# Windowed attention into a two-layer feed-forward block: V loaded and shifted by pairs, weights after it, y products 24 slots behind

## The chip, the cores and the metric

The kernel runs on one core of a Trainium2 chip. The metric is the device time in microseconds of one execution. TensorE (PE, with its weight loads on PEld), VectorE (DVE), ScalarE (ACT) and GpSimd (POOL) run their own instruction streams in order; SyncE (SP) and POOL issue the transfers here, each in its own queue order. SP's transfers form queue q1 of the profile, POOL's form queue q0, and both run on the core's 16 DMA engines.

## The reference

For 8 batches, 8 heads, 576 positions and a head size of 64 (inputs in float32):

```python
scores = scale * np.matmul(q, k.transpose(0, 1, 3, 2))
rel = pos[:, None] - pos[None, :]
mask = (rel >= 0) & (rel < window)          # window = 64
attn = softmax(np.where(mask, scores, -1e9))
attn_out = np.matmul(attn, v)
x = attn_out.transpose(0, 2, 1, 3).reshape(B * S, H * D)   # 4608 x 512
h = x @ w_in                                # 512 -> 2048
g = h - np.tanh(h)
y = g @ w_out                               # 2048 -> 512
```

## The kernel before

**Attention.** A pair g is two heads of one batch (heads pr and pr + 4 of batch b, g = 4b + pr), so there are 32 pairs. Every window of 64 queries sees its own 64 keys and the 64 before it, so 9 windows make a pair. For each pair SP loads q and k (`load_qk`, 288 KB each), an engine casts them to bf16 (`cast_qk`, on POOL but for pair 0), PE transposes them (`tr`, tiles `tp`), ACT and DVE copy the transposes out (`qt`, `kt`), PE makes the scores in three groups of three windows (`scores`, `sp`), ACT takes the exponential (`pt`), DVE multiplies by the mask, PE multiplies by V in three groups (`pv`, tile `ov`), and DVE normalises into `xs` (`rc`, then two multiplications for each group). After every second pair PE transposes two pairs' `xs` (`x_tr`, tile `tpx`, first windows 0 to 3, then 4 to 8) and DVE copies them into `xT`, the input of the first layer. `tp` and `tpx` share a pool of two PSUM buffers.

**V.** A tile `vw` for one batch (two such tiles, batches take turns) holds on partitions 64 to 127 the V rows of a window and on partitions 0 to 63 those of the window before. `load_v` fills the upper half from DRAM with a cast to bf16, in two transfers on POOL's queue, in pieces of 64 elements (128 B); `shift_v` copies the upper half to the lower, one window further, on SP's queue. No `pv` group can finish before both.

**Feed-forward.** The 4608 tokens are 9 chunks of 512 and d_ff is 16 tiles of 128. For chunk c and tile m, `hp_mm` makes four matmuls (`hp`), ACT the tanh (`th`) and DVE the difference (`gT`). `yp_mm` makes four matmuls of the second layer (`yp`); four of these make 128 tokens of output, which ACT copies (`ysb`, `y_out`) and SP stores. `yp` has one PSUM buffer.

**Order.** Everything is written out by half-slots h; slot n is half-slots 2n and 2n + 1. An even half-slot holds one `hp_mm`, an odd one a `yp_mm`; the attention's pieces are put at half-slots by tables (`TIGHT` for batches 0 and 1, `WIDE` for the rest), counted from a start a that depends on the pair. Slots 0 to 143 hold the first layer's 9 x 16 `hp_mm`; the second layer runs 16 slots behind it (slots 16 to 159). All of batch 0's attention stands ahead of slot 0, batch 1's pairs start at half-slots 8, 12, 16 and 20 (its first `pv` in slot 7), and batch 2's pairs at half-slots 20, 28, and so on.

**Start.** POOL issues in this order: V of batch 0 (pair 0, then pairs 1 to 3 together), the four quarters of w_in among the casts of pairs 1 to 3, the four quarters of w_out, V of batch 1, V of batch 2, then the casts of the following pairs. SP issues q and k of pairs 0 to 3, the shift of batch 0 (pair 0, then the rest), q and k of later pairs, the shift of batch 1 in one transfer. A transfer waits on its queue until the transfer eight places ahead on that queue has landed, since eight semaphores take turns.

Of the kernel before, what the change touches and what calls it, by code (L numbers as in the profile page):

```python
# [15 lines left out]
def kernel(  # L16
# [9 lines left out]
    nc = tc.nc  # L26
    B, H, S, D = q.shape
    NP = H // 2
# [7 lines left out]
    NC = NT // TOK  # L36
    M = d_ff // 128
# [2 lines left out]
    ctx.enter_context(tc.manual_schedule())  # L40

    const = ctx.enter_context(tc.tile_pool(name="const", bufs=1))
    qk_pool = ctx.enter_context(tc.tile_pool(name="qk", bufs=5))
    row_pool = ctx.enter_context(tc.tile_pool(name="row", bufs=3))
    sm_pool = ctx.enter_context(tc.tile_pool(name="sm", bufs=3))
    xt_pool = ctx.enter_context(tc.tile_pool(name="xt", bufs=3))
    g_pool = ctx.enter_context(tc.tile_pool(name="g", bufs=2))
    ps_hp = ctx.enter_context(tc.tile_pool(name="ps_hp", bufs=2, space=PSUM))
    ps_yp = ctx.enter_context(tc.tile_pool(name="ps_yp", bufs=1, space=PSUM))
    ps_tp = ctx.enter_context(tc.tile_pool(name="ps_tp", bufs=2, space=PSUM))  # L50
# [4 lines left out]
    mask = const.tile([128, 64], BF16, name="mask")  # L55
    w_in_sb = const.tile([128, 4, d_ff], BF16, name="w_in_sb")
    w_out_sb = const.tile([128, M, d_model], BF16, name="w_out_sb")
# [17 lines left out]
    def cast(eng, g, n):  # L75
        t = row_pool.tile([P, E, 2, D], BF16, tag=n + "b", name=n + "b")
        o = t.rearrange("p e h d -> p h e d")
        i = stage.pop((g, n)).rearrange("p h (e d) -> p h e d", d=D)
        if eng is nc.scalar:
            nc.scalar.activation(o, i, ACT.Copy)  # L80
        else:
            eng.tensor_copy(o, i)  # L82
        rows[g, n] = t

    def cast_qk(g):
        cast(nc.gpsimd, g, "q")
        cast(nc.gpsimd, g, "k")

    def load_v(b, p0=0, p1=NP):
        for i in range(2):  # L90
            nc.gpsimd.dma_start(  # L91
                out=vw[b % NV][64:128, p0:p1, :, 64 * i:64 * i + 64].rearrange("p r j d -> p (r j) d"),
                in_=v[b, NP * i + p0:NP * i + p1].rearrange("h (j p) d -> p (h j) d", p=64))

    def shift_v(b, p0=0, p1=NP):
        w = vw[b % NV].rearrange("p r j c -> p r (j c)")
        nc.sync.dma_start(out=w[0:64, p0:p1, 129:], in_=w[64:128, p0:p1, :(NJ - 1) * 129])


    for g in range(NP):  # L100
        load_qk(g)
# [7 lines left out]
    for i in range(NR):  # L109
        nc.vector.memset(qT[i], 0.0)  # L110
        nc.vector.memset(kT[i][:, 0:64], 0.0)
    nc.gpsimd.memset(mask, 1.0)

    nc.gpsimd.affine_select(mask, mask, compare_op=ALU.is_ge, fill=0.0,
                            base=-1, pattern=[[-1, 8], [-8, 8]], channel_multiplier=1)
    nc.gpsimd.affine_select(mask, mask, compare_op=ALU.is_ge, fill=0.0,
                            base=64, pattern=[[1, 8], [8, 8]], channel_multiplier=-1)
    w_in_r = moe_w_in.rearrange("(ko ki) f -> ki ko f", ki=128)
    w_out_r = moe_w_out.rearrange("(ko ki) f -> ki ko f", ki=128)

    def load_w_in(i):
        nc.gpsimd.dma_start(out=w_in_sb[:, :, 512 * i:512 * i + 512],
                            in_=w_in_r[:, :, 512 * i:512 * i + 512])

    def load_w_out(i):
        nc.gpsimd.dma_start(out=w_out_sb[:, 4 * i:4 * i + 4, :], in_=w_out_r[:, 4 * i:4 * i + 4, :])

    cast(nc.scalar, 0, "q")
    cast(nc.vector, 0, "k")
    load_v(0, 1, NP)  # L130
    load_w_in(0)
    cast_qk(1)
    load_w_in(1)
    cast_qk(2)
    load_w_in(2)
    load_w_in(3)
    cast_qk(3)
    for i in range(4):
        load_w_out(i)
    load_v(1)  # L140
    shift_v(0, 0, 1)
    shift_v(0, 1, NP)

    xT = {}

# [64 lines left out]
    def hp_mm(c, m):  # L210
        hp = ps_hp.tile([128, TOK], F32, tag="hp", name="hp")
        for ki in range(4):
            nc.tensor.matmul(hp, w_in_sb[:, ki, m * 128:(m + 1) * 128], chunk_tile(c)[:, ki, :],  # L213
                             start=(ki == 0), stop=(ki == 3))
        th = sm_pool.tile([128, TOK], F32, tag="th", name="th")
        nc.scalar.activation(th, hp, ACT.Tanh)  # L216
        return hp, th

    def g_sub(c, m, hp, th):
        if m == 0:  # L220
            gT[c] = g_pool.tile([128, M, TOK], BF16, tag="gT", name="gT")
        nc.vector.tensor_tensor(gT[c][:, m, :], hp, th, ALU.subtract)  # L222

    def yp_mm(c, st):
        s, part = divmod(st, 4)
        if part == 0:
            yps[c, s] = ps_yp.tile([128, d_model], F32, tag="yp", name="yp")
        for i in range(4):
            m = 4 * part + i
            nc.tensor.matmul(yps[c, s], gT[c][:, m, s * 128:(s + 1) * 128], w_out_sb[:, m, :],  # L230
                             start=(m == 0), stop=(m == M - 1))

    def y_out(c, s):
        ysb = sm_pool.tile([128, d_model], F32, tag="ysb", name="ysb")
        nc.scalar.activation(ysb, yps[c, s], ACT.Copy)  # L235
        for u in range(2):
            r0 = c * TOK + s * 128 + 64 * u
            nc.sync.dma_start(out=out[r0:r0 + 64, :].rearrange("(a e) d -> e a d", e=E),
                              in_=ysb[64 * u:64 * u + 64, :])
# [3 lines left out]
    items = {}  # L243

    def at(h, *fn):
        items.setdefault(h, []).append(fn)

    NG = B * NP
    WIDE = dict(q=0, k=1, s0=4, s1=4, s2=6, mask=8, v0=10, v1=13, v2=15, x0=17, x1=19)
    TIGHT = dict(q=0, k=1, s0=3, s1=3, s2=4, mask=5, v0=6, v1=7, v2=8, x0=10, x1=11)  # L250
    at_v2 = {}
    for g in range(NG):
        b, pr = divmod(g, NP)
        o = TIGHT if b < 2 else WIDE
        a = 3 * g - 21 if b == 0 else 4 * g - 8 if b == 1 else 8 * g - 44
        if b > 0:
            at(a - 24, load_qk, g)
            at(a - 8, cast_qk, g)
        at(a + o["q"], tr, g, "q")
        at(a + o["k"], tr, g, "k")  # L260
        for i in range(3):
            at(a + o[f"s{i}"], scores, g, i)
        at(a + o["mask"], masking, g)
        for i in range(3):
            at(a + o[f"v{i}"], pv, g, i)
        at_v2[g] = a + o["v2"]
        if pr % 2 == 1:
            at(a + o["x0"], x_tr, b, pr // 2, 0, 4)
            at(a + o["x1"], x_tr, b, pr // 2, 4, NJ)
    at(6, shift_v, 1)  # L270
    for b in range(2, B):
        a = at_v2[NP * (b - 1) - 1] + 1
        at(a, load_v, b)
        at(a + 22, shift_v, b)

    for h in range(min(items), 2 * 16 * (NC + 1) + 2):
        n = h // 2
        c, m = divmod(n, M)
        if h % 2 == 0:
            cy, sy = divmod(n - 17, M)  # L280
            if n >= 17 and sy % 4 == 3 and cy < NC:
                y_out(cy, sy // 4)
            if 0 <= c < NC:
                hidden = hp_mm(c, m)
        elif 1 <= c <= NC:
            yp_mm(c - 1, m)
        for fn in items.get(h, []):
            fn[0](*fn[1:])
        if h % 2 == 0 and 0 <= c < NC:
            g_sub(c, m, *hidden)  # L290
# [29 lines left out]
```

## Time and profile before

| | us |
|---|---|
| median of 3 runs | 415.07 |
| lowest, highest | 413.35, 416.54 |
| the profiled execution, whole | 415.04 |
| its span, first to last instruction | 413.3 |

The span holds 328.9 us of PE busy time, 241.5 of DVE, 185.5 of ACT and 90.7 of POOL. The profile's clock row lies at 0.5 to 0.9 of full speed in several slices up to about 124 us and at full speed after that. How to read it: PE is busy for 80% of the span, but a share over the whole span mixes the load-bound start, the middle and the tail; the sections below go by stretches.

### The profile page before, as it was taken

The page shows a single profiled execution, that of the slowest core. Times are in us where ns is not written, and L with a number is a line of the kernel's source. Part 1 is how long each engine was busy: PE and PEld are TensorE (multiplying, and loading weights), DVE is VectorE, ACT ScalarE, POOL GpSimd, SP SyncE. Part 2 cuts the span into 40 slices and gives each one's busy share as a digit, 9 for nine tenths or more (in the row PEclk, how much of TensorE's full clock was granted, in tenths as well). Part 3 has the DMA queues.
Part 4 walks back from the last instruction along what each step waited for, and adds up shares of the span by engine and source line. Part 5 has one row for each costly group of instructions (what it writes and reads, how often), then busy time and mean ns, then how long its engine had stood idle before and what let it go on. Part 6 is the DMA issues. An engine that isn't in the chain of part 4 may idle for free.

```text
span 413.3 us, 6323 instructions
## 1 busy us (share of the span) xinstructions
PE 328.9 (80%) x2384; PEld 179.0 (43%) x2384; DVE 241.5 (58%) x553; ACT 185.5 (45%) x342; POOL 90.7 (22%) x97
## 2 busy tenths in 40 slices
PE   3024580056779999998999999999999999999984
PEld 2023340034335555554555555555555544444431
DVE  4116741057867777777778777877777753333300
ACT  4113151034626655564555656565565434444411
POOL 8721181012142141306123240612200000000000
PEclk9999797558989999999999999999999999999999
DMA  9999999985092499369547935994300110101021
GB/s 163 146 161 255 201 186 60 86 143 135 2 57 84 116 132 113 89 158 113 143 107 150 112 96 139 128 135 107 93 27 26 41 37 30 49 27 51 27 75 51
DMA packets 58765, 41.84 MB, mean 101 GB/s; under 512 B 38768, under 2 KB 42864, under 8 KB 58736
## 3 DMA queue, kind: packets, MB, share of 16 engines
q0 software_dynamic: 41376, 8.91, 76.4%
q1 hardware_dynamic: 17360, 32.54, 30.7%
q8 instruction: 18, 0.29, 0.3%
q14 instruction: 11, 0.09, 0.1%
HBM read 36.70 MB, written 9.44 MB: 112 GB/s over the span
## 4 chain that ended last, share of the span: by engine, by line
PE 64%; DMA 18%; DVE 9%; ACT 4%; issue 2%; POOL 1%; ACTq 0%; SPq 0%; POOLq 0%
PE yp L230 27%; PE hp L213 26%; DMA vw<-in_v_dram 10%; DMA w_in_sb<-in_moe_w_in_dram 5%; PE ov L183 4%; PE sp L170 3%; DMA vw<-vw 3%; PE tp L156 3%; DVE xs L189 2%; DVE pt L176 2%; DVE gT L222 2%; ACT th L216 2%; DVE qt L161 2%; ACT qt L160 1%; POOL vw L91 1%
## 5 line engine op out<-in xcount | busy, mean ns | idle before, releaser
L213 PE MATMUL hp<-xT,w_in_sb 128*128 128x512 bf16 x576 | 152.4, 387 | 4.0 <-DVE xT L203 2.9
L230 PE MATMUL yp<-w_out_sb,gT 128*128 128x512 bf16 x576 | 146.7, 380 | 2.8 <-ACT ysb L235 2.8
L222 DVE TENSOR_TENSOR gT<-hp,th 128x512 bf16<-128x512 f32 x144 | 99.5, 692 | 71.6 <-ACT th L216 70.1
L216 ACT ACTIVATE th<-hp 128x512 f32<-128x512 f32 x144 | 86.0, 597 | 119.2 <-PE hp L213 95.5
L183 PE MATMUL ov<-vw,pt 128*128 128x129 bf16 x288 | 35.5, 235 | 56.5 <-DMA vw<-vw 21.5
L213 PEld LDWEIGHTS <-w_in_sb 128*128 128x128 bf16 x576 | 52.8, 100 | 53.0 <-issue 9.7
L230 PEld LDWEIGHTS <-gT 128*128 128x128 bf16 x576 | 52.2, 98 | 50.3 <-issue 4.4
L189 DVE TENSOR_TENSOR xs<-ov,rc 64x192 bf16<-64x192 f32 x192 | 68.1, 355 | 4.6
L172 ACT ACTIVATE pt<-sp 128x384 bf16<-128x384 f32 x96 | 43.3, 488 | 54.9 <-PE sp L170 54.6
L183 PEld LDWEIGHTS <-pt 128*128 128x128 bf16 x288 | 23.8, 103 | 80.8 <-issue 47.1
L82 POOL CAST qb<-qf 72x1024 bf16<-72x1024 f32 x31 | 33.3, 1074 | 107.1 <-DMA qf<-in_q_dram 52.3
L186 DVE RECIPROCAL rc<-ov 128x3 f32<-128x3 f32 x96 | 17.1, 178 | 55.9 <-PE ov L183 53.4
L91 POOL DMA_DIRECT2D vw<-in_v_dram x18 | 19.7, 1099 | 87.1 <-PE ov L183 73.2
L235 ACT ACTIVATE ysb<-yp 128x512 f32<-128x512 f32 x36 | 21.5, 597 | 27.4 <-PE yp L230 27.4
L82 POOL CAST kb<-kf 72x1024 bf16<-72x1024 f32 x31 | 32.3, 1041 | 2.3 <-DMA kf<-in_k_dram 1.4
L170 PE MATMUL sp<-qt,kt 128*128 128x128 bf16 x288 | 29.8, 237 | 1.5 <-ACT kt L163 1.1
L170 PEld LDWEIGHTS <-kt 128*128 128x128 bf16 x288 | 23.3, 107 | 13.7 <-ACT kt L163 1.8
L176 DVE TENSOR_TENSOR pt<-pt,mask 128x1152 bf16<-128x1152 bf16 x32 | 28.1, 877 | 0.9
L163 ACT ACTIVATE kt<-tp 128x576 bf16<-128x576 bf16 x32 | 20.6, 649 | 17.2 <-PE tp L156 17.2
L161 DVE COPY qt<-tp 64x576 bf16<-64x576 bf16 x32 | 14.7, 460 | 13.2 <-ACT qt L160 13.0
L156 PE MATMUL tp<-ident,kb 72*128 72x72 bf16 x256 | 14.8, 205 | 7.9 <-DVE qt L161 6.9
L160 ACT ACTIVATE qt<-tp 64x576 bf16<-64x576 bf16 x32 | 20.2, 634 | 1.1 <-PE tp L156 1.1
(24 smaller groups left out, 96.3 us busy)
## 6 DMA issues: line engine op xcount, KB each, us to landing
qf<-in_q_dram SPq DMA_DIRECT2D x32, 288.0 KB
kf<-in_k_dram SPq DMA_DIRECT2D x32, 288.0 KB
out_dram<-ysb SPq DMA_DIRECT2D x72, 128.0 KB
vw<-in_v_dram POOLq DMA_DIRECT2D x14, 288.0 KB, 10.8
vw<-vw SPq DMA_DIRECT2D x7, 516.0 KB
w_in_sb<-in_moe_w_in_dram POOLq DMA_DIRECT2D x4, 512.0 KB, 22.3
w_out_sb<-in_moe_w_out_dram POOLq DMA_DIRECT2D x4, 512.0 KB, 36.0
vw<-in_v_dram POOLq DMA_DIRECT2D x2, 216.0 KB, 19.1
```

The costliest lines, as they stand in the source:

```text
L82: eng.tensor_copy(o, i)
L156: nc.tensor.transpose(tp[:, e, :], src[:, e, :], ident[:P, :P])
L160: nc.scalar.activation(o[0:64, :, 0], t[0:64], ACT.Copy)
L170: nc.tensor.matmul(sp[:, i, :], kT[g % NR][:, 64 * j:64 * j + 128], qT[g % NR][:, j].rearrange("c h t -> c (h t)"), start=True, stop=True)
L172: nc.scalar.activation(PT[g % NR][:, 3 * grp:3 * grp + 3, :], sp, ACT.Exp, scale=scale)
L176: nc.vector.tensor_tensor(p, p, mask.unsqueeze(1).to_broadcast([128, 2 * NJ, 64]), ALU.mult)
L183: nc.tensor.matmul(ov[:, i, :], PT[g % NR][:, j, :], vw[b % NV][:, pr, j, :], start=True, stop=True)
L189: nc.vector.tensor_tensor(xs[b % 2][r, 3 * grp:3 * grp + 3, pr, :], ov[r, :, r], rc[r].to_broadcast([64, 3, 64]), ALU.mult)
L213: nc.tensor.matmul(hp, w_in_sb[:, ki, m * 128:(m + 1) * 128], chunk_tile(c)[:, ki, :], start=(ki == 0), stop=(ki == 3))
L216: nc.scalar.activation(th, hp, ACT.Tanh)
L222: nc.vector.tensor_tensor(gT[c][:, m, :], hp, th, ALU.subtract)
L230: nc.tensor.matmul(yps[c, s], gT[c][:, m, s * 128:(s + 1) * 128], w_out_sb[:, m, :], start=(m == 0), stop=(m == M - 1))
```

## The change

- V of batches 0 and 1 is loaded pair by pair (two transfers of 72 KB for each pair) and shifted pair by pair (129 KB each).
- POOL's order becomes: V pairs 0 and 1 of batch 0, casts of pair 1, V pair 2, casts of pair 2, V pair 3, w_in 0, casts of pair 3, w_in 1 to 3, V of batch 1 by pairs, and then w_out's quarters after the casts of pairs 4, 5, 6 and 7.
- The second layer runs 24 slots behind the first (`LAG`), so `gT` has three buffers; the q and k load buffers go from five to four.
- From batch 2 on every pair starts 4 half-slots earlier, and the two `x_tr` pieces stand at a + 19 and a + 22 (before: a + 17 and a + 19).

```diff
-    qk_pool = ctx.enter_context(tc.tile_pool(name="qk", bufs=5))
+    qk_pool = ctx.enter_context(tc.tile_pool(name="qk", bufs=4))
-    g_pool = ctx.enter_context(tc.tile_pool(name="g", bufs=2))
+    g_pool = ctx.enter_context(tc.tile_pool(name="g", bufs=3))
...
     cast(nc.scalar, 0, "q")
     cast(nc.vector, 0, "k")
-    load_v(0, 1, NP)
+    load_v(0, 1, 2)
...
+    cast_qk(1)
+    load_v(0, 2, 3)
+    cast_qk(2)
+    load_v(0, 3, 4)
     load_w_in(0)
-    cast_qk(1)
-    load_w_in(1)
-    cast_qk(2)
-    load_w_in(2)
-    load_w_in(3)
     cast_qk(3)
-    for i in range(4):
-        load_w_out(i)
-    load_v(1)
-    shift_v(0, 0, 1)
-    shift_v(0, 1, NP)
+    for i in range(1, 4):
+        load_w_in(i)
+    for pr in range(NP):
+        shift_v(0, pr, pr + 1)
...
-    WIDE = dict(q=0, k=1, s0=4, s1=4, s2=6, mask=8, v0=10, v1=13, v2=15, x0=17, x1=19)
+    WIDE = dict(q=0, k=1, s0=4, s1=4, s2=6, mask=8, v0=10, v1=13, v2=15, x0=19, x1=22)
...
-        a = 3 * g - 21 if b == 0 else 4 * g - 8 if b == 1 else 8 * g - 44
-        if b > 0:
+        a = 3 * g - 21 if b == 0 else 4 * g - 8 if b == 1 else 8 * g - 48
+        if b > 1:
             at(a - 24, load_qk, g)
             at(a - 8, cast_qk, g)
...
-    at(6, shift_v, 1)
+
+    for pr in range(NP):
+        at(-20 + pr, load_qk, NP + pr)
+        at(-16 + pr, load_v, 1, pr, pr + 1)
+        at(-8 + 4 * pr, cast_qk, NP + pr)
+        at(6 + 3 * pr, shift_v, 1, pr, pr + 1)
+        at(-7 + 4 * pr, load_w_out, pr)
...
+    LAG = 16 + 8
-    for h in range(min(items), 2 * 16 * (NC + 1) + 2):
+    for h in range(min(items), 2 * (16 * NC + LAG) + 2):
...
-            cy, sy = divmod(n - 17, M)
-            if n >= 17 and sy % 4 == 3 and cy < NC:
-                y_out(cy, sy // 4)
+            if sy % 4 == 0 and 0 < n - LAG <= 16 * NC:
+                y_out(*divmod((n - LAG) // 4 - 1, 4))
...
-        elif 1 <= c <= NC:
-            yp_mm(c - 1, m)
+        elif 0 <= cy < NC:
+            yp_mm(cy, sy)
```

On POOL, at the end of the start: vw_94 is the V tile of batches 0 and 2, vw_95 that of batch 1; the unmarked row is the load of batch 2 (x2, x8: so many like it in a row).

```order
-L126 DMA w_out_sb<-in_moe_w_out_dram 128x4x512 x4
-L91 DMA vw_95<-in_v_dram 64x36x64 x2
+L103 DMA w_in_sb<-in_moe_w_in_dram 128x4x512 x3
+L91 DMA vw_95<-in_v_dram 64x9x64 x8
+L82 CAST qb<-qf 72x2x8x64
+L82 CAST kb<-kf 72x2x8x64
+L107 DMA w_out_sb<-in_moe_w_out_dram 128x4x512
+L82 CAST qb<-qf 72x2x8x64
+L82 CAST kb<-kf 72x2x8x64
+L107 DMA w_out_sb<-in_moe_w_out_dram 128x4x512
 L91 DMA vw_94<-in_v_dram 64x36x64 x2
```

V of batch 1 moved from behind w_out to ahead of it, and two quarters of w_out and the casts of pairs 4 and 5 now stand between it and V of batch 2; the casts of pairs 6 and 7 stay behind V of batch 2.

On SP, at the shift of batch 1: the first four rows with + are q and k of pairs 9 and 10 around the shift of pair 0, and the last three are the shifts of pairs 1 to 3; in brackets what a transfer waits for (DMASW are POOL's transfers, DMAHW are SP's, Pool_49 a cast on POOL).

```order
-L97 DMA vw_95<-vw_95 64x4x1032 [waits DMAHW6_49,DMASW5_49,DMASW4_49]
+L72 DMA qf<-in_q_dram 72x2x512 [waits DMAHW6_49,Pool_49]
+L72 DMA kf<-in_k_dram 72x2x512 [waits DMAHW7_49,Pool_49]
+L97 DMA vw_95<-vw_95 64x1032 [waits DMAHW0_49,DMASW5_49,DMASW4_49]
+L72 DMA qf<-in_q_dram 72x2x512 [waits DMAHW1_49,Pool_49]
+L72 DMA kf<-in_k_dram 72x2x512 [waits DMAHW2_49,Pool_49]
+L97 DMA vw_95<-vw_95 64x1032 [waits DMAHW3_49,DMASW7_49,DMASW6_49]
+L97 DMA vw_95<-vw_95 64x1032 [waits DMAHW4_49,DMASW1_49,DMASW0_49]
+L97 DMA vw_95<-vw_95 64x1032 [waits DMAHW5_49,DMASW3_49,DMASW2_49]
```

The shift became four, and the loads of pair 10 now stand between the first and the other three; with four load buffers those loads wait for the casts of pair 6.

On DVE, in the steady stretch, from one pair's mask to the second copy into `xT`; first before:

```order
L176 TENSOR_TENSOR pt_96<-pt_96,mask 128x1152
L161 COPY qt_103<-tp 64x9x64
L222 TENSOR_TENSOR gT<-hp,th 128x512
L203 COPY xT<-tpx 128x2x256
L186 RECIPROCAL rc<-ov 128x3
L189 TENSOR_TENSOR xs_105<-ov,rc 64x3x64 x2
L222 TENSOR_TENSOR gT<-hp,th 128x512
L203 COPY xT<-tpx 128x2x320
```

and here the same place of the changed kernel:

```order
L174 TENSOR_TENSOR pt_96<-pt_96,mask 128x1152
L159 COPY qt_103<-tp 64x9x64
L220 TENSOR_TENSOR gT<-hp,th 128x512
L184 RECIPROCAL rc<-ov 128x3
L187 TENSOR_TENSOR xs_105<-ov,rc 64x3x64 x2
L220 TENSOR_TENSOR gT<-hp,th 128x512
L201 COPY xT<-tpx 128x2x256
L220 TENSOR_TENSOR gT<-hp,th 128x512
L184 RECIPROCAL rc<-ov 128x3
L187 TENSOR_TENSOR xs_105<-ov,rc 64x3x64 x2
L201 COPY xT<-tpx 128x2x320
```

The copies out of `tpx` moved one and two half-slot groups away from the mask and from the copy out of `tp`, which take buffers of the same pool.

## Rows read from the trace of the kernel before

**Rows 1.** The page: engines' busy time; chain that ended last; one costly group.
```profile
PE 328.9 (80%) x2384; PEld 179.0 (43%) x2384; DVE 241.5 (58%) x553; ACT 185.5 (45%) x342; POOL 90.7 (22%) x97
...
PE yp L230 27%; PE hp L213 26%; DMA vw<-in_v_dram 10%; DMA w_in_sb<-in_moe_w_in_dram 5%; PE ov L183 4%; PE sp L170 3%; DMA vw<-vw 3%; PE tp L156 3%; DVE xs L189 2%; DVE pt L176 2%; DVE gT L222 2%; ACT th L216 2%; DVE qt L161 2%; ACT qt L160 1%; POOL vw L91 1%
...
L222 DVE TENSOR_TENSOR gT<-hp,th 128x512 bf16<-128x512 f32 x144 | 99.5, 692 | 71.6 <-ACT th L216 70.1
```
**Rows 2.** Stretches: start:end, length, each engine's busy time (instructions), clock, DMA, GB/s.
```profile
0.00:50.80 50.80, 15.76 (x154) 12.68 (x155) 20.76 (x59) 12.57 (x22) 20.97 (x30) 0.96 1.70 185
...
61.80:87.20 25.40, 2.51 (x22) 1.41 (x19) 3.62 (x9) 2.05 (x5) 2.02 (x2) 0.61 2.89 85
87.20:100.40 13.20, 9.68 (x85) 6.22 (x84) 7.96 (x21) 7.00 (x14) 3.22 (x4) 0.72 0.76 171
100.40:115.20 14.80, 10.02 (x101) 5.67 (x98) 12.88 (x31) 7.78 (x15) 4.33 (x5) 1.00 0.18 13
115.20:136.60 21.40, 19.22 (x138) 10.20 (x138) 14.84 (x37) 10.03 (x19) 7.35 (x7) 0.92 1.60 60
136.60:390.60 254.00, 247.35 (x1769) 132.26 (x1768) 175.73 (x391) 137.23 (x253) 43.61 (x42) 1.00 0.85 91
390.60:413.30 22.70, 14.53 (x65) 6.13 (x63) 0.58 (x1) 2.98 (x5) 0.00 (x0) 0.97 0.18 58
```
**Rows 3.** Such stretches, first-layer matmuls (L213) alone: PE, PEld, clock, DMA, GB/s.
```profile
61.80:87.20 25.40, 1.03 (x4) 0.32 (x5) 0.61 2.89 85
87.20:100.40 13.20, 5.13 (x12) 1.55 (x12) 0.72 0.76 171
```
**Rows 4.** The chain that ended last, in order of time: start, length, what.
```profile
31.41 42.11 DMA vw<-in_v_dram
73.57 11.27 DMA vw<-vw
```
**Rows 5.** Timeline of PE: start, length, operation, count, idle before it and releaser.
```profile
28.37 0.37 PE L183 MATMUL ov<-vw,pt 128*128 128x129 bf16 x2 [10.54 <-DMA vw<-vw]
...
34.39 0.51 PE L183 MATMUL ov<-vw,pt 128*128 128x129 bf16 x3 [1.82 <-DVE pt L176]
...
84.88 0.38 PE L183 MATMUL ov<-vw,pt 128*128 128x129 bf16 x2 [10.96 <-DMA vw<-vw]
```
**Rows 6.** Timeline of POOL.
```profile
49.78 2.29 POOL L91 DMA_DIRECT2D vw<-in_v_dram  x2 [17.22 <-PE ov L183]
52.06 1.06 POOL L82 CAST qb<-qf 72x1024 bf16<-72x1024 f32 x1
```
**Rows 7.** Timeline of SP's queue.
```profile
17.58 9.52 SPq L97 DMA_DIRECT2D vw<-vw  x2
```
**Rows 8.** DMA queues from 17 to 24 us: packets, MB, share of 16 engines.
```profile
q0 software_dynamic: 1952, 0.49, 409.2%
q1 hardware_dynamic: 16, 0.03, 2.8%
```
**Rows 9.** DMA queues from 24 to 31 us.
```profile
q0 software_dynamic: 1186, 1.18, 117.1%
```
**Rows 10.** DMA queues from 62 to 74 us.
```profile
q0 software_dynamic: 5181, 0.68, 377.2%
```
**Rows 11.** Waits of PE from 136.6 to 390.6 us: total, times, longest.
```profile
PE tp L156 <- DVE qt L161: 5.5, 10, 1.0
PE hp L213 <- DVE xT L203: 1.1, 2, 0.6
```
**Rows 12.** One batch's 16 slots in the steady stretch; columns as in Rows 2.
```profile
173.40:210.60 37.20, 35.30 (x286) 19.76 (x284) 28.66 (x67) 21.23 (x41) 10.37 (x10) 1.00 1.37 123
```
**Rows 13.** Timeline of PE at chunk 1's first slot and in the tail.
```profile
117.39 0.81 PE L213 MATMUL hp<-xT,w_in_sb 128*128 128x512 bf16 x3 [1.78 <-DVE xT L203]
...
395.67 3.61 PE L230 MATMUL yp<-w_out_sb,gT 128*128 128x512 bf16 x16 [0.69 <-ACT ysb L235]
399.96 3.61 PE L230 MATMUL yp<-w_out_sb,gT 128*128 128x512 bf16 x16 [0.69 <-ACT ysb L235]
```

More of the change, by code (lines that the diff above doesn't have):

```diff
@@ L97, in shift_v, with load_w_in, load_w_out @@
         nc.sync.dma_start(out=w[0:64, p0:p1, 129:], in_=w[64:128, p0:p1, :(NJ - 1) * 129])
+    w_in_r = moe_w_in.rearrange("(ko ki) f -> ki ko f", ki=128)
+    w_out_r = moe_w_out.rearrange("(ko ki) f -> ki ko f", ki=128)
+    def load_w_in(i):
+        nc.gpsimd.dma_start(out=w_in_sb[:, :, 512 * i:512 * i + 512],
+                            in_=w_in_r[:, :, 512 * i:512 * i + 512])
+    def load_w_out(i):
+        nc.gpsimd.dma_start(out=w_out_sb[:, 4 * i:4 * i + 4, :], in_=w_out_r[:, 4 * i:4 * i + 4, :])
     for g in range(NP):
@@ L111 @@
         nc.vector.memset(kT[i][:, 0:64], 0.0)
+    cast(nc.scalar, 0, "q")
+    cast(nc.vector, 0, "k")
+    load_v(0, 1, 2)
     nc.gpsimd.memset(mask, 1.0)
@@ L117 @@
                             base=64, pattern=[[1, 8], [8, 8]], channel_multiplier=-1)
[L118 to L129, printed above, removed]
-    load_v(0, 1, NP)
-    load_w_in(0)
-    cast_qk(1)
-    load_w_in(1)
-    cast_qk(2)
-    load_w_in(2)
-    load_w_in(3)
-    cast_qk(3)
-    for i in range(4):
-        load_w_out(i)
-    load_v(1)
-    shift_v(0, 0, 1)
-    shift_v(0, 1, NP)
+    cast_qk(1)
+    load_v(0, 2, 3)
+    cast_qk(2)
+    load_v(0, 3, 4)
+    load_w_in(0)
+    cast_qk(3)
+    for i in range(1, 4):
+        load_w_in(i)
+    for pr in range(NP):
+        shift_v(0, pr, pr + 1)
     xT = {}
@@ L274 @@
         at(a + 22, shift_v, b)
-    for h in range(min(items), 2 * 16 * (NC + 1) + 2):
+    LAG = 16 + 8
+    for h in range(min(items), 2 * (16 * NC + LAG) + 2):
         n = h // 2
         c, m = divmod(n, M)
+        cy, sy = divmod(n - LAG, M)
         if h % 2 == 0:
-            cy, sy = divmod(n - 17, M)
-            if n >= 17 and sy % 4 == 3 and cy < NC:
-                y_out(cy, sy // 4)
+            if sy % 4 == 0 and 0 < n - LAG <= 16 * NC:
+                y_out(*divmod((n - LAG) // 4 - 1, 4))
             if 0 <= c < NC:
                 hidden = hp_mm(c, m)
-        elif 1 <= c <= NC:
-            yp_mm(c - 1, m)
+        elif 0 <= cy < NC:
+            yp_mm(cy, sy)
         for fn in items.get(h, []):
```

## The prediction

> **What bounds the kernel now.** I read the page's shares first: PE is busy for 80% of the span, yet the chain that ended last goes through transfers of V for 13% of it [rows 1]. So I cut the span into stretches at the first-layer matmuls, four of which make a slot [rows 2, 3]. The reader is to see four regimes. Up to 50.8 us PE mostly waits for batch 0's V and then for the chain of attention steps. In 61.8 to 87.2 us stands a hole: 25.4 us in which one slot (slot 7, four matmuls) gets done. From 87.2 to 115.2 us eight slots pass, three at a clock of 0.72 (4.4 us each, part of it at 1.2 GHz after the idle time) and five at full clock (2.96 us each), where DVE is busy for 12.88 of 14.8 us. From 136.6 to 390.6 us PE has 247.35 us of work in 254.0: that is PE-bound, and only work or waits of PE itself count there.
>
> The hole is read from the chain in order of time: batch 1's V, the last transfer in POOL's order after w_in and w_out, stands there from 31.41 for 42.11 us, and its shift for 11.27 us more [rows 4]; PE sat before `ov` until 84.88 [rows 5].
>
> **The change part by part.** The sum is made against the profiled execution (415.04 us, of which 413.3 is span, so 1.74 lies around it); its whole time is the median of the runs shown within 0.1 us.
>
> *V of batch 1 ahead of w_out.* w_out is 4 x 512 rows of 1 KB, 2048 packets. Between 24 and 31 us q0 moved 1186 such packets in 7 us [rows 9], so w_out alone costs 12.1 us of the queue, and up to twice that where q1's loads share the engines half and half. Batch 1's V is 64 x 36 x 2 = 4608 packets of 128 B; at the 5181 in 12 us of [rows 10] that is 10.7 us. So V lands 12 to 24 us before 73.5, between 49.5 and 61.4 us, where slot 7 wants pair 0 at 61.8. Its shift waits on SP behind the loads of pairs 8 and 9, thus for the casts of pairs 4 and 5, which now stand ahead of V of batch 2 on POOL: about 49 us. The nearest row for a 129 KB shift is batch 0's, issued at 17.58 and used at 28.37 [rows 5, 7], 10.8 us: pair 0 is there at about 60. The shifts of pairs 1 to 3 stand behind the loads of pair 10, those behind the casts of pair 6, those behind V of batch 2, which POOL can issue only when PE has finished batch 0 (49.78, 2.29 long); two casts at 1.06 later [rows 6] it is 54.2, and plus 10.8 the shifts land at 65. PE wants pair 1 two slots after pair 0, at 61.8 + 2 x 2.96 = 67.7. So the wait that is left is between nothing and, with these shifts queued until V of batch 2 has gone through (the 84.88 of before less half of w_out, 6 us, which now comes later: 79), 11 us. I take 3, nearer to the small shift's own row. Slot 7 itself costs 2.96. Term: 25.4 - 2.96 = 22.4 saved, 3 given back.
>
> *Clock after the hole.* Without it slots 8 to 10 run like slots 11 to 15: 13.2 - 3 x 2.96 = 4.3 saved (nothing, if PE still idles).
>
> *V and shifts of batch 0 by pairs.* Nothing: the same packets precede the first shift in q0, and between 17 and 24 us q1 got 16 packets against 1952 [rows 8]. From 28.37 on the attention chain sets the pace; pair 1's `pv` waited for its mask, not for its shift [rows 5]. Bounds: a first shift that lands as soon as it is issued would save up to 8, four shifts one after another would cost 15 (both below as rivals). w_in lands later in q0's order than before but is wanted only at 50.8.
>
> *Batch 2 four half-slots earlier.* Half a pair more falls into slots 7 to 15. A steady batch has 28.66 us of DVE in 16 slots [rows 12], 16 x 0.69 of it `gT` [rows 1], so 4.4 a pair; 2.2 more at a busy share of 87% costs 2.5. The same half pair leaves the PE-bound stretch: a batch's PE work of 35.30 [rows 12] less 128 layer matmuls at 3.61 / 16 each [rows 13] (28.9) is 6.4, an eighth is 0.8 saved.
>
> *The second layer 24 slots behind.* Slots 16 to 23 lose their `yp`, and took 21.4 us [rows 2]. DVE then needs 28.66 / 16 x 8 = 14.3, at 87% 16.5; the wait for `xT` at chunk 1's first slot, 1.78 [rows 13], stays: 18, so 3.4 saved (0 to 7.1). The tail gets eight more slots of `yp` alone, two groups at 399.96 - 395.67 = 4.29 [rows 13]: 8.6 lost. w_out, now last, is wanted some 40 us after it can land.
>
> *x transposes moved.* In the PE-bound stretch nearly all the idle time, 5.5 + 1.1 of 6.65 us, is PE waiting for a `tp` buffer that DVE has not emptied, or for `xT` [rows 2, 11]; the order on DVE shows both copies out of `tpx` moved clear of it. 5 saved (0 to 6.6).
>
> *Buffers.* The third `gT` and the fourth load buffer cost no instruction; what the missing fifth does is the wait on casts priced above.
>
> Sum: -22.4 + 3 - 4.3 + 2.5 - 0.8 - 3.4 + 8.6 - 5 = -21.8. Span 391.5, and with the 1.74 around it a time of **393**.
>
> A rule of the Trainium skill speaks about the first and the third part. The row first: with a shift of 64 packets issued at 17.58, q1 moved 16 packets in 17 to 24 us while q0 moved 1952 [rows 8], and the shift came through only at 28.37. The Trainium skill ("DMA: Bandwidth & Descriptors", Queues, rings and completion order) says that each DMA engine goes round robin between the queues it has work for, a packet at a time. By that, a small shift would pass a long V load within a few us, in this kernel and in the one before; the rows of before do not agree, so I leave it only the small chance of the second rival.
>
> **The rivals.**
> 1. *The shifts of pairs 1 to 3 stay behind V of batch 2.* For it: the 516 KB shift of before, issued at 73.57, came through after 11.27 us with batch 2's V on q0 [rows 4], and [rows 8]. Against: the second shift of batch 0, issued 9.52 us after 17.58, had let pair 1 go by 34.39 [rows 5, 7], so a shift behind large packets is quick. The wait is 11 instead of 3, and the idle time brings the lower clock back (4.3): 393 + 8 + 4.3 = **405**.
> 2. *The small shifts pass at once.* Then `pv` of batch 0 starts up to 8 us earlier, and no wait is left: **385**. Against: [rows 8].
> 3. *V of batch 1 gains nothing*, since eight of its transfers each wait for the one eight places ahead on POOL's queue, down to the last quarter of w_in, and the q and k loads take the engines that w_out leaves. Then most of the hole stays: 22.4 and 4.3 are not saved, and nor is the 3 lost: 393 + 23.7 = 416.7; with half of w_out out of the way, 6, about **411**. Against: w_in's rate in [rows 9].
> 4. *The other side: each 129 KB shift costs 10.8 us and they run one after another.* Place: SP's queue in batch 0. The fourth would land at 28.4 + 3 x 10.8 = 60.8, and a pair takes 34.39 - 28.37 = 6.0 us [rows 5], so slot 0 moves from 50.8 to 66.8: +16. In batch 1 pair 0's shift would land at 71.6 and the others 10.8 apart, the last at 104, where it is wanted at 66.8 + 11 + 6 x 2.96 = 96 (+8), and with the lower clock (4.3) it is 393 + 16 + 8 + 4.3 = **421**. It decides from 6 us a shift on, where they become slower than the pairs' own pace. Against: the 387 KB shift of before took under 34.39 - 27.1 = 7.3 us [rows 5, 7].
>
> **How the numbers follow.** Forecast 0.70 (own range 385 to 400), rival 1 0.17, rival 2 0.05, rival 3 0.05, rival 4 0.03. The likeliest time is 393. From the forecast's lower part and rival 2 up to and including rival 1 the range is 384 to 408. A measurement of this kernel can tell about 1% from no change, so faster means under 410.9: the forecast, rivals 1 and 2, 0.92. Rival 3 and its neighbours give 0.05 within 1%; rival 4 gives 0.03 slower.
>
> **What would show it.** Right: in the changed trace PE's wait before `ov` for V is under some 5 us in all after slot 0, slots 7 to 15 take about 2.9 to 3.2 us each at full clock, slot 0 starts within 2 us of 50.8, the waits of `tp` for `qt` in the steady stretch shrink to under 2 us, and the tail after the last `hp` is 31 us. Wrong: a wait before `ov` of 8 us or more with V of batch 2 in q0 (rival 1), slot 0 before 46 (rival 2) or after 58 (rival 4), or a new wait for `gT`, `w_out_sb` or the casts, which would break the sum.

## The result and the profile after

The changed kernel takes 397.4 us (median of four runs, 396.17 to 398.24) against 415.13 of the kernel before, beside it: a ratio of 0.957, 95% interval 0.953 to 0.962. It is faster, by 17.7 us where 22 were forecast. The profiled execution took 396.17 us with a span of 392.9, 1.4 more than the span of 391.5 in the sum. It is the quickest of the four (the spans of the others are 395.2 to 395.7), which matters for one stretch below. In the tables that follow, times are medians of all four runs of a kernel, and ratios leave out a run that is more than 1.5% above its kernel's quickest: one run each of the kernel with the old x transposes and of the one with 16 slots of lag and w_out behind V of batch 2, two of the latter with fillers.

The stretches of the changed kernel, cut where those of before were cut [rows 2] and finer where it went another way; columns: start:end, length, busy time of PE, PEld, DVE, ACT and POOL (instructions), granted clock, DMA, GB/s:
```profile
51.10:62.10 11.00, 9.56 (x71) 4.42 (x70) 5.18 (x10) 5.83 (x11) 7.20 (x8) 1.00 1.92 151
62.10:69.00 6.90, 2.47 (x23) 1.47 (x20) 3.71 (x9) 2.12 (x6) 2.02 (x2) 0.86 1.35 193
69.00:81.90 12.90, 10.97 (x92) 7.09 (x91) 7.49 (x19) 7.28 (x15) 4.57 (x4) 0.55 2.26 136
...
88.20:97.00 8.80, 2.25 (x19) 0.98 (x16) 5.17 (x13) 1.73 (x4) 0.00 (x0) 0.85 0.87 163
...
102.60:117.30 14.70, 11.80 (x112) 6.81 (x110) 13.71 (x35) 9.21 (x20) 8.39 (x8) 1.00 2.59 109
117.30:361.60 244.30, 244.30 (x1751) 130.81 (x1750) 176.58 (x386) 135.59 (x250) 46.24 (x42) 1.00 0.71 89
361.60:392.90 31.30, 21.90 (x97) 9.26 (x95) 0.69 (x1) 4.18 (x7) 0.00 (x0) 0.97 0.18 59
```
Slot 7, 25.4 us before, takes 6.9. Slots 8 to 10, in 69.0 to 81.9, run mostly at the lower granted clock (0.55 on average) and take 12.9, hardly less than the 13.2 of before. Slot 13, 88.2 to 97.0, is a new small hole. In the long stretch from slot 24 on PE is busy all but without a gap.

Two transfers of V are still on the chain of work that ended last (start, length, what), and PE waits for them twice:
```profile
50.30 16.33 DMA vw<-vw
86.61 8.60 DMA vw<-vw
```
```profile
66.68 0.28 PE L181 MATMUL ov<-vw,pt 128*128 128x129 bf16 x2 [1.41 <-DMA vw<-vw]
95.25 0.38 PE L181 MATMUL ov<-vw,pt 128*128 128x129 bf16 x2 [2.30 <-DMA vw<-vw]
```
The first is the shift of pair 0 of batch 1, in slot 7, where the kernel before waited 10.96 us in one piece [rows 5]. It took 16.33 us from issue to landing, issued behind q and k loads of its own queue. The second, in slot 13, is the shift of batch 2, which nothing in the sum had.

### The profile page after: what moved, and what is told of

It is laid out like the page before. It is cut to its first block, busy times and chain, and to the rows that moved or that the text cites. A ratio compares the mean times of both kernels' runs of the same rounds, so it can differ in the third digit from the quotient of the medians.

```text
span 392.9 us, 6368 instructions
## 1 busy us (share of the span) xinstructions
PE 329.2 (84%) x2384; PEld 179.7 (46%) x2384; DVE 244.2 (62%) x553; ACT 184.8 (47%) x342; POOL 99.7 (25%) x107
## 4 chain that ended last, share of the span: by engine, by line
PE 72%; DMA 13%; DVE 4%; issue 3%; POOL 3%; ACT 3%; SPq 0%; POOLq 0%; ACTq 0%
PE yp L228 32%; PE hp L211 29%; DMA vw<-vw 6%; DMA w_in_sb<-in_moe_w_in_dram 5%; PE ov L181 4%; PE sp L168 3%; PE tp L154 3%; DMA kf<-in_k_dram 2%; DVE xs L187 1%; PE tpx L193 1%; POOL kb L82 1%; DVE gT L220 1%; ACT ysb L233 1%; POOL vw L91 1%; ACT th L214 1%
## 5 line engine op out<-in xcount | busy, mean ns | idle before, releaser
L228 PE MATMUL yp<-w_out_sb,gT 128*128 128x512 bf16 x576 | 145.0, 379 | 4.3 <-ACT ysb L233 4.3
L181 PE MATMUL ov<-vw,pt 128*128 128x129 bf16 x288 | 36.5, 240 | 41.7 <-DMA vw<-vw 12.9
L170 ACT ACTIVATE pt<-sp 128x384 bf16<-128x384 f32 x96 | 43.3, 489 | 32.1 <-PE sp L168 31.9
L82 POOL CAST qb<-qf 72x1024 bf16<-72x1024 f32 x31 | 34.7, 1121 | 74.2 <-DMA qf<-in_q_dram 49.5
L91 POOL DMA_DIRECT2D vw<-in_v_dram x28 | 25.7, 924 | 68.4 <-PE ov L181 55.0
L82 POOL CAST kb<-kf 72x1024 bf16<-72x1024 f32 x31 | 34.0, 1096 | 20.9 <-DMA kf<-in_k_dram 20.1
L184 DVE RECIPROCAL rc<-ov 128x3 f32<-128x3 f32 x96 | 17.1, 178 | 34.0 <-PE ov L181 31.3
L174 DVE TENSOR_TENSOR pt<-pt,mask 128x1152 bf16<-128x1152 bf16 x32 | 30.3, 946 | 0.9
L161 ACT ACTIVATE kt<-tp 128x576 bf16<-128x576 bf16 x32 | 20.7, 648 | 7.3 <-PE tp L154 7.3
L159 DVE COPY qt<-tp 64x576 bf16<-64x576 bf16 x32 | 14.7, 460 | 13.1 <-ACT qt L158 12.8
L154 PE MATMUL tp<-ident,qb 72*128 72x72 bf16 x256 | 14.9, 208 | 5.7 <-POOL mask L127 5.7
```

Of the source, the lines that this page charges most:

```text
L91: nc.gpsimd.dma_start(out=vw[b % NV][64:128, p0:p1, :, 64 * i:64 * i + 64].rearrange("p r j d -> p (r j) d"), in_=v[b, NP * i + p0:NP * i ...
L154: nc.tensor.transpose(tp[:, e, :], src[:, e, :], ident[:P, :P])
L170: nc.scalar.activation(PT[g % NR][:, 3 * grp:3 * grp + 3, :], sp, ACT.Exp, scale=scale)
L174: nc.vector.tensor_tensor(p, p, mask.unsqueeze(1).to_broadcast([128, 2 * NJ, 64]), ALU.mult)
L181: nc.tensor.matmul(ov[:, i, :], PT[g % NR][:, j, :], vw[b % NV][:, pr, j, :], start=True, stop=True)
```

## The experiments

Each edit is one against the changed kernel unless the text says otherwise. Slot times come from each kernel's profiled execution; where some matmul records are missing, slots were counted by the `Tanh` that ends each. One trace a kernel is a thin base for a single slot: the kernels with the lag at 16 and with the old x transposes run the same program up to slot 15 as the changed kernel, and show 8.9 and 8.8 us for slot 7 and 6.3 and 7.5 for slot 13, where the changed kernel's trace has 6.9 and 8.8.

### Which half of the change to V of batch 1 closes the hole

w_out ahead of V of batch 1 again, V still by pairs:
```
-        at(-7 + 4 * pr, load_w_out, pr)
+        at(-18, load_w_out, pr)
```


> The changed kernel with one thing undone: w_out's four quarters are issued ahead of V of batch 1 again, all else (pairs, lag, starts, x transposes) as changed. Theory A (the gain is the place of V of batch 1 in POOL's queue): V of batch 1 lands after 70 us again, PE waits in slot 7 for 12 to 20 us more than in the changed kernel, and the time is 408 to 418. Theory B (the gain comes from the pairs or from the later second layer): within 3 us of the changed kernel's 397.4.

V of batch 1 loaded and shifted whole, still ahead of w_out:
```
-        at(-16 + pr, load_v, 1, pr, pr + 1)      # in the loop over pr
-        at(6 + 3 * pr, shift_v, 1, pr, pr + 1)
+    at(-16, load_v, 1)                           # once
+    at(6, shift_v, 1)
```


> The changed kernel with V of batch 1 loaded in one piece (two transfers of 288 KB) and shifted in one piece (516 KB), both at the place in the queues where pair 0's stood. Theory A (place, not pairs: the first small shift was held behind the loads of pairs 8 and 9 on SP's queue, so it came no earlier than a whole shift would): 395 to 400, and PE's first wait for the shift ends at 64 to 69 us. Theory B (pairs matter): the wait in slot 7 grows by 5 us or more, 402 or more.

Both edits at once:

> The changed kernel with both halves of its change to V of batch 1 undone: w_out is issued ahead of V of batch 1, and V of batch 1 is loaded and shifted whole; the rest (lag, x transposes, batch 2's place, batch 0 by pairs, four load buffers) stays. With the order alone undone the hole of slot 7 was 13.5 us, with the pairs alone undone 15.9, with neither undone 6.9. Theory A (the two halves shorten the same wait one after the other, and add up): 22 to 24 us in slot 7, 405 to 412. Rival B (what is left over, the load buffers and batch 0's order, has taken most of the hole by itself): 14 to 18 us in slot 7, 399 to 404. Rival C (V whole behind w_out lands as in the kernel before, 73.5 us, and its shift of 11 us follows with the same 25.4 us): over 24 us, 412 or more.

| V of batch 1 | slot 7, us | time, us | ratio to before |
|---|---|---|---|
| whole, behind w_out | 27.6 | 411.97 | 0.988 (0.982 to 0.993) |
| whole, ahead of w_out | 15.9 | 402.5 | 0.964 (0.954 to 0.974) |
| by pairs, behind w_out | 13.5 | 400.59 | 0.963 (0.955 to 0.971) |
| by pairs, ahead of w_out | 6.9 | 397.4 | 0.957 (0.953 to 0.962) |

PE's waits around slot 7 (total, times, longest) with w_out first, with V whole, and with both:
```profile
PE ov L181 <- DMA vw<-vw: 7.6, 1, 7.6
```
```profile
PE ov L181 <- DMA vw<-vw: 10.2, 1, 10.2
```
```profile
PE ov L181 <- DMA vw<-in_v_dram: 13.2, 1, 13.2
PE ov L181 <- DMA vw<-vw: 10.6, 1, 10.6
```
With both undone the hole of before is back whole (25.4 there), the load and then the shift, as theory C of that run had it (27.6 us in slot 7; the time, 411.97, lies where the ranges of A and C meet). So these two edits are what closes it; everything else in the change is worth 1.2% by itself. Each half alone takes 12 to 14 us out of the hole, both some 19 to 21: they overlap. Theory A of the first run, which gave the order nearly everything, fell: with V by pairs its place behind w_out costs some 5 to 7 us of hole (its profiled execution, at 404.2, was the slowest of its four) and some 3 us of time, which the intervals do not tell from nothing. With V whole and early the hole is 9 us longer, as theory B of the second run had it; its interval overlaps with the changed kernel's too.

### What holds slot 13

w_out issued behind V of batch 2 on POOL:
```
-        at(-7 + 4 * pr, load_w_out, pr)
+        at(-1 + 2 * pr, load_w_out, pr)
```


> The changed kernel with w_out issued behind V of batch 2 on POOL instead of ahead of it, nothing else. Theory A (the 8.8 us of slot 13 are V of batch 2 landing late because w_out stands before it in q0): V of batch 2 then lands some 6 us sooner than 86.5, its shift is through before pair 0 of batch 2 wants it, slot 13 goes back to 3 us, and the idle time and the lower clock behind it go as well: 390 to 393. Rival B (V of batch 2 waits for PE's last matmuls on batch 0's tile and then takes as long whatever stands before it, or its shift of 8.6 us is what counts): slot 13 stays at 7 us or more, 395 to 399. Rival C (w_out now comes too late for the second layer, which begins in slot 24, or the shift of V of batch 2 shares its engines with w_out): a new wait before yp or before ov, 399 or more.

A third tile for V (`NV, NR = 3, 3`), so that V of batch 2 needn't wait for PE to leave batch 0's; the first load of V moves up into the loop that clears the tiles:

> The changed kernel with a third tile for V, so that V of batch 2 need not wait for PE's last matmuls on batch 0's, nor V of batch 3 for those on batch 1's; nothing else. Theory A (slot 13's 8.8 us come from V of batch 2 being issued only once PE has left batch 0's tile, and the masks of 3 us near 101 to 110 us of other runs from casts that POOL does in a burst after it has waited for V of batch 3's tile): slot 13 goes back to 3 us, no mask over 2 us after 100 us, 388 to 393. Rival B (V of batch 2 is held up by w_out and by the q and k loads in the queues, not by its tile): slot 13 stays at 6 us or more, 395 to 398. Rival C (V of batch 2, issued earlier, now stands in the way of V of batch 1's last pairs or their shifts): a longer slot 7, 398 or more.

w_out's place gives 393.61 us, ratio 0.945 (0.940 to 0.950), its interval clear of the changed kernel's; the tile gives 396.69, 0.952 (0.944 to 0.959), no difference. In the first the shift of batch 2 was issued on SP's queue at 78.12 instead of 86.61, and PE waits for no V at all from slot 7 on. In the second V of batch 2 and its shift stand on the chain after all:
```profile
78.12 0.66 SPq L97 DMA_DIRECT2D vw<-vw  x1
```
```profile
51.20 34.13 DMA vw<-in_v_dram
85.38 11.95 DMA vw<-vw
```
So it was no wait for the tile. V of batch 2 is issued near 50 us either way, behind two quarters of w_out, and takes 34 us or more to land. With the third tile PE waited 7.1 us for the shift and slot 13 grew to 13.4 us, so rival B of that run (6 or more) holds. How long PE waits there differs much among the six traces with w_out ahead of V of batch 2 and slot 7 short: nothing with the lag at 16, 1.0, 1.6 and 2.3 us in others, 5.8 with the order of batch 0 as before, and that 7.1. V of batch 2 landed at 83.3 to 86.5 us in those six, and at 77.7 to 80.7 in the four with w_out behind it, where the wait is nothing three times and 0.7 once. Slot 13 fell to 6.0 us with w_out out of the way, not to 3 as theory A had it. What is left there is DVE (PE's timeline of that kernel, last bracket: idle before, releaser):
```profile
90.12 0.35 PE L181 MATMUL ov<-vw,pt 128*128 128x129 bf16 x3 [2.10 <-DVE pt L174]
91.51 0.35 PE L181 MATMUL ov<-vw,pt 128*128 128x129 bf16 x3 [1.04 <-DVE xs L187]
92.98 0.41 PE L181 MATMUL ov<-vw,pt 128*128 128x129 bf16 x3 [1.12 <-DVE xs L187]
```
Three `pv` groups stand in one slot: two of pair 7 and, with batch 2 four half-slots earlier, the first of pair 8. Each waits for DVE.

### The clock after the hole

Two extra matmuls, whose result nothing reads, in every second half-slot of slots 0 to 15, in the changed kernel and in the one with 16 slots of lag and w_out behind V of batch 2 (next part):
```
+    warm = ps_yp.tile([128, d_model], F32, tag="yp", name="warm")
...
+        elif 0 <= n < 16:
+            for fill in range(2):
+                nc.tensor.matmul(warm, w_in_sb[:, fill, 0:128], chunk_tile(0)[:, fill, :], start=True, stop=True)
```


> The changed kernel with two extra matmuls of 512 columns, whose result nothing reads, in every second half-slot of slots 0 to 15 (work added that the reference does not want; the output is unchanged). They give PE something to do where it waits. Theory A (slots 8 to 10 took 12.9 us instead of 8.9 because PE ran them at the lower granted clock of 1.2 GHz from 67.1 to 80.7 us, after the idle time of slot 7): the granted clock stays higher in 67 to 81 us, and 3 to 5 us are won, less the time of the fillers themselves where PE does not wait (up to 16 x 2 x 0.2 = 7 us): 394 to 399 with slots 8 to 10 at or under 11 us. Rival B (these slots are paced by DVE and the attention chain, and the clock only goes with it): slots 8 to 10 stay at 12.9 us or grow, at a higher clock or not, and the time is 398 to 403.

> As the kernel with 16 slots and w_out behind V of batch 2, with the two extra matmuls in every second half-slot of slots 0 to 15 (their result is read by nothing). Theory A (the lower granted clock in slots 8 to 10 costs time by itself): 2 to 4 us less than without them, 382 to 385. Rival B (the chain of attention steps and DVE set the pace there): the same or up to 3 us more, 386 to 390.

395.02 us, ratio 0.949 (0.942 to 0.956), and 388.25, 0.923 (0.912 to 0.934) against 387.88, 0.928 (0.919 to 0.937) without fillers. Neither differs beyond its interval, and the fillers' own time is in these numbers, so the whole time settles little (395.02 lies in theory A's range, 388.25 in rival B's); the slots say more. In the first, slots 8 to 10 ran at a mean clock of 0.90 and took 10.9 us instead of 12.9:
```profile
68.00:78.90 10.90, 8.99 (x95) 5.41 (x96) 7.22 (x19) 7.18 (x15) 4.57 (x4) 0.90 2.34 129
```
In the second pair the time at the lower clock fell from 17.1 to 6.8 us before slot 24, and slots 8 to 10 took 11.4 instead of 11.6. Two kernels without fillers say the same: with the order of batch 0 as before the lower clock ended at 69.6 us and with the third tile at 70.4, instead of 80.7, and slots 8 to 10 took 10.9 and 10.8 us. The first of the two, in those slots:
```profile
66.90:77.80 10.90, 8.19 (x93) 5.14 (x92) 7.31 (x19) 7.19 (x15) 4.57 (x4) 0.88 1.76 166
```
So the clock is worth about 2 us in these slots, and 10.9 is about what they need with most of them at full clock. They hold more than the slots of before that the forecast took as their measure. PE's matmuls of the first layer and with transposes of q and k (`tp`) in slots 8 to 10 of the changed kernel, and its transposes (`tpx` are those of x) in slots 11 to 15 of the kernel before:
```profile
L211 PE MATMUL hp<-xT,w_in_sb 128*128 128x512 bf16 x12 | 5.7, 633 | 0.0
...
L154 PE MATMUL tp<-ident,kb 72*128 72x72 bf16 x24 | 1.6, 231 | 0.7 <-DVE qt L159 0.7
L154 PE MATMUL tp<-ident,qb 72*128 72x72 bf16 x24 | 1.6, 236 | 0.0
```
```profile
L195 PE MATMUL tpx<-ident,xs 128*128 128x128 bf16 x18 | 1.6, 218 | 0.3
L156 PE MATMUL tp<-ident,kb 72*128 72x72 bf16 x16 | 0.8, 197 | 0.1
L156 PE MATMUL tp<-ident,qb 72*128 72x72 bf16 x8 | 0.4, 196 | 0.0
```
That is 48 transposes in three slots against 42 in five, 24 of them of q and k. The first-layer matmul at 633 ns in the mean, 379 in slots 11 to 15 of before at full clock, shows the clock's part.

### The lag of the second layer

`LAG = 16` instead of 24, in the changed kernel; the same with w_out behind V of batch 2; and that with `LAG = 14`:

> The changed kernel with the second layer 16 slots behind the first again, all else as changed. Theory A (the lag buys only cover for w_out, which lands by 92 us and is wanted at about 103): the tail loses 8.6 us, slots 16 to 23 become 17.5 to 19 us instead of 14.7, so 4 to 6 us faster, 392 to 394. Theory B (the 24 slots are needed: PE waits for w_out, or slots 16 to 23 grow by as much as the tail shrinks): 396 to 402.

> The changed kernel with the second layer 16 slots behind the first as before, and w_out issued behind V of batch 2. Alone the first edit gave 390.1 and the second 393.6 (changed kernel 397.4). Theory A (the lag costs its slots in the tail, less what it gives slots 16 to 23; w_out's place costs the wait of slot 13; they lie in different stretches and add up): 385 to 388, with a tail of about 23 us after the last first-layer matmul and no wait for V's shift after 80 us. Rival B (with the second layer beginning 8 slots earlier, w_out behind V of batch 2 comes too late for it): a wait before yp near slot 16, 389 to 394.

> As the kernel beside it with w_out behind V of batch 2, but with the second layer 14 slots behind the first instead of 16. Theory A (a slot of lag costs its second-layer work in the tail, about 1.07 us a slot by the 8.6 us that 8 slots cost, and slots 14 and 15 have room on PE, which waits there for DVE anyway): 1.5 to 2.5 us less than with 16 slots, 383 to 386. Rival B (slots 14 and 15 are then as full as slots 16 to 23 were, so what leaves the tail comes back there, as with slots 16 to 23 of the kernel before, or the last gT of a chunk is not ready when the second layer wants it): the same time or more, 386 to 390.

| lag, w_out | time, us | ratio to before | slots 14 to 23, us | after the last `hp`, us |
|---|---|---|---|---|
| 24, ahead of V of batch 2 | 397.4 | 0.957 (0.953 to 0.962) | 20.3 | 31.9 |
| 16, ahead | 390.08 | 0.938 (0.931 to 0.945) | 24.9 | 23.2 |
| 24, behind | 393.61 | 0.945 (0.940 to 0.950) | 22.3 | 31.9 |
| 16, behind | 387.88 | 0.928 (0.919 to 0.937) | 24.0 | 23.2 |
| 14, behind | 382.94 | 0.917 (0.909 to 0.924) | 25.9 | 20.6 |

Eight slots of lag cost 7.3 us in one pair and 5.7 in the other by the medians, 8 and 7 by the ratios, more than the 4 to 6 of theory A of the first run; the tail alone shrinks by 8.7. How much of it slots 14 to 23 take back these traces don't settle: 20.3 us is the lowest of nine kernels with a lag of 24, which took 20.3 to 25.9 there. The two edits add up (theory A, at 387.9). The last two slots of lag gave 5 us, more than the 2 expected, with intervals that overlap; its profile shows 2.5 of it in the tail, and a wait of 2.2 us for the shift of batch 3 that the kernel with 16 slots has near slot 30 and this one has not. At 382.94 us it is the fastest kernel of the study, 8.3% below the kernel before and some 14 us below the changed one.

### The x transposes, and the order of batch 0

`x0=17, x1=19` as before:

> The changed kernel with the two x transposes of a batch at a + 17 and a + 19 again. Theory A (they cost PE a wait for a transpose buffer at 12 places): 5 to 7 us slower, 402 to 405, with PE's waits of tp for qt in the steady stretch back at 4 to 6 us. Theory B (the steady stretch got shorter for another reason): within 2 us of 397.4.

406.29 us, ratio 0.972 (0.963 to 0.981): the place of the transposes is worth some 9 us by the medians and 6 by the ratios, more than the 5 of the sum; from slot 24 to the last `hp` the two traces differ by 7.1. The wait that the sum named is back behind slot 16:
```profile
PE tp L154 <- DVE qt L159: 7.6, 11, 2.1
```
The order of batch 0 as before (V in two pieces, w_in and casts between them, two shifts):

> The changed kernel with V of batch 0, its shifts, w_in and the casts of batch 0 in the order of the kernel before (pair 0's quarter of V first, then the rest in one, shift of pair 0, then one shift of the other three); V of batch 1 stays by pairs and ahead of w_out. Theory A (the order of batch 0 moves nothing, as the sum had it): slot 0 starts within 2 us of 51.1, 395 to 400. Rival B (the order of batch 0 is what lets V of batch 1 go out early, since the transfers of V wait on POOL's queue for those eight places ahead): the hole of slot 7 grows by 4 us or more, 401 to 408. Rival C (batch 0 by pairs delays the casts and with them slot 0): slot 0 starts 2 us or more earlier, 391 to 395.

399.07 us, ratio 0.958 (0.951 to 0.964): no difference. Slot 0 starts at 50.8, as theory A had it, and the hole of slot 7 didn't grow (5.2 us). Slot 13 took 12.3 us in this trace, with a wait of 5.8 for the shift of batch 2; whether the order of batch 0 makes that longer, one trace doesn't show.

## Why the prediction was right, and where its sum was not

The time lies in the range and the sign is right. By the steps of the prediction, in us of span:

| step | forecast | measured | off by |
|---|---|---|---|
| slot 0 starts (batch 0 by pairs) | 50.8 | 51.1 | +0.3 |
| slot 7 | 2.96 + 3 | 6.9 | +0.9 |
| slots 8 to 10 | 8.9 | 12.9 | +4.0 |
| slots 11 to 15 | 14.8 + 2.5 | 20.7 | +3.4 |
| slots 16 to 23 | 18 | 14.7 | -3.3 |
| slot 24 to the last `hp` | 248.2 | 244.3 | -3.9 |
| tail, from 361.6 | 31.3 | 31.3 | 0 |

- **V of batch 1.** The mechanism and the size hold. With both halves undone slot 7 takes 27.6 us, with both in place 6.9. The wait for the shift is 1.41; the rest of the 3 given back is a mask (1.90) and the `ov` steps. The shift itself was mis-sized: it took 16.33 us and landed at 66.6, where the sum had 10.8 and 60; that PE had to wait for its mask until 65.04 hides most of this. Rival 1 didn't come: the shifts of pairs 1 to 3 let nobody wait. Nor did rival 2, since that shift didn't pass at once. Rivals 3 and 4 are excluded by slot 7 and slot 0.
- **Batch 0.** The term of nothing came out at 0.3, in part by chance: a mask of 2.61 us stands in front of slot 0 in this trace (last section). Seven other kernels with V of batch 0 by pairs, without a mask over 1.9 us there, start slot 0 at 48.0 to 49.7.
- **Clock after the hole.** This term, 4.3 saved, failed. The clock still fell, from 67.1 to 80.7 us, behind a slot in which PE was busy for 2.47 of 6.9 us. And full clock gives only 2 of the 4.3, since slots 11 to 15 of before were the wrong measure: they hold some 8 transposes a slot, slots 8 to 10 hold 16. So the sign that the prediction named, 2.9 to 3.2 us each for slots 7 to 15, was missed.
- **Batch 2 earlier, and what w_out does to it.** The 2.5 for half a pair more is near the 2.9 that slot 13 grows without any wait for V (6.0 against 3.1 in the kernel before). What failed is a term that was never written. The prediction asked when w_out is wanted, and found 40 us to spare; it did not ask when V of batch 2, behind w_out in q0, is wanted. In the kernel before it stood behind w_out too and landed at 81.72, but was first wanted in slot 15, after 111 us; in the changed kernel it landed at 86.47 and is wanted in slot 13, at 92.7. The price with its shift is 2.8 us in slot 13 of these two traces, and 3.8 of the median when w_out goes behind it.
- **Lag.** 8.6 lost in the tail is what the tails show. The forecast of 18 us for slots 16 to 23 looks 3.3 too high in this trace alone: of the eight other kernels with a lag of 24 seven took 17.2 to 19.8 there, each with a mask of about 3 us in that stretch (last section) that this execution happened not to have, and the eighth, without such a mask, 14.9. With a lag of 16 they took 18.5 to 19.8. The net cost, 5.2 in the sum, measured 7.3 and 5.7 by the medians, 8 and 7 by the ratios: of the 8.7 lost in the tail some 1 to 3 come back ahead of it, where the sum had 3.4.
- **x transposes.** Right in place, undersized. PE's waits of 6.65 us in the steady stretch fell to 0.3:
```profile
PE ov L181 <- DVE xs L187: 0.3, 1, 0.3
```
  The work left in it fell by 3.05 us (247.35 to 244.30), where the sum had 0.8 for the half pair that moved ahead; what the rest is isn't shown.

So the sum came out only 1.4 us off because rows that were too hopeful by 8.6 us in all were nearly balanced by two that were too careful by 7.2. That it held so closely is partly luck, and of the quickest execution: the median is 4.4 us over the 393 forecast. The sign and most of the size rest on the hole, which the experiments confirm.

## What to carry to other kernels

When a transfer is moved down a queue because it isn't wanted yet, look at what is queued behind it as well as at when it is wanted itself: here w_out's last quarter landed at 91.59, 25 us before the second layer starts, and its place still cost 4 us through V of the next batch. Take as the measure for a stretch that is to run faster a stretch with the same work in it, counted by instructions. Here work of the second layer that was moved later reappeared in the tail in full, so undo such a delay once the thing it made room for is fixed.

## What the runs showed of the hardware

A mask on DVE, 0.758 us in the median, took up to 5.2 us in these traces when POOL ran casts back to back beside it. DVE and then POOL in the changed kernel with a lag of 14 and w_out behind V of batch 2, and PE behind them (start, length, operation, in brackets idle before and releaser):
```profile
42.73 4.98 DVE L174 TENSOR_TENSOR pt<-pt,mask 128x1152 bf16<-128x1152 bf16 x1
```
```profile
42.39 0.73 POOL L91 DMA_DIRECT2D vw<-in_v_dram  x1 [4.35 <-DMA w_in_sb<-in_moe_w_in_dram]
43.11 1.05 POOL L82 CAST qb<-qf 72x1024 bf16<-72x1024 f32 x1
44.09 1.05 POOL L82 CAST kb<-kf 72x1024 bf16<-72x1024 f32 x1
45.07 1.04 POOL L82 CAST qb<-qf 72x1024 bf16<-72x1024 f32 x1
46.06 1.03 POOL L82 CAST kb<-kf 72x1024 bf16<-72x1024 f32 x1
```
```profile
47.77 0.51 PE L181 MATMUL ov<-vw,pt 128*128 128x129 bf16 x3 [6.04 <-DVE pt L174]
```
The mask ends at 47.71, 0.62 us after the last of four casts (47.09). All 18 masks over 1.9 us in the traces of the changed kernel and the experiments end 0.61 to 0.62 us after the end of some cast. The changed kernel has one: 2.61 us at 43.38, beside two casts from 43.35 to 45.38, and PE waited 3.68 us for it in front of slot 0. In 12 of the 18 a cast's record begins before the mask's. In the other six, the one shown among them, the mask's begins 0.17 to 0.66 us before the first cast, while POOL issues a load of V, and the mask waits all the same. Where the mask came first and POOL issued nothing, a cast gave way: in the changed kernel a cast that began 0.01 us behind a mask took 1.65 us instead of 1.05, and the mask its usual time (DVE, then POOL):
```profile
111.75 0.76 DVE L174 TENSOR_TENSOR pt<-pt,mask 128x1152 bf16<-128x1152 bf16 x1
```
```profile
111.75 1.65 POOL L82 CAST qb<-qf 72x1024 bf16<-72x1024 f32 x1 [3.40 <-issue]
```
The Trainium skill ("SBUF — State Buffer", Who interferes with whom) says that a VectorE instruction with two SBUF inputs contends with a GpSimd instruction that reads SBUF, through a port pair that is an exclusive lock, and that the order of issue decides who blocks. The traces agree that either can hold up the other, and for the order in all but the six cases above; they add that casts issued back to back can keep the mask out for all four of them. That the casts cause it was not tried by an experiment that moves them; it rests on these end times.

POOL's issuing of a load goes with longer masks too. In all 14 traces 72 masks begin while POOL issues one and meet no cast: 46 took their usual 0.76 us, 26 took 1.46 to 1.64. The 213 with nothing on POOL beside them took 0.75 to 0.76. One of the 26, in the changed kernel (DVE, then POOL):
```profile
161.88 1.60 DVE L174 TENSOR_TENSOR pt<-pt,mask 128x1152 bf16<-128x1152 bf16 x1
```
```profile
161.22 2.29 POOL L91 DMA_DIRECT2D vw<-in_v_dram  x2 [5.71 <-PE ov L181]
```
What decides between the two is not shown.

Whether a mask meets a run of casts moves these times by a few us: slot 0 starts at 52.3 to 53.3 in the three traces with a mask of about 5 us in front of it, at 51.1 and 51.3 in the two with one of 2.6 to 2.8, and at 48.0 to 50.8 in the other eight of the changed kernel and its experiments. It may be a part of the spread among the runs of one kernel; only one execution of each was profiled, so that is not shown.
